# Attention before a mixture of experts: q and k split on GpSimd and turned by one DMA transpose a pair

## The chip, the cores and the metric

The kernel runs on one core of one Trainium2 chip. The metric is the device time of one execution in microseconds; lower is better. The core's engines are PE (TensorE, matmul; its weight loads are listed apart as PEld), DVE (VectorE), ACT (ScalarE), GpSimd (POOL in the rows) and SP (SyncE, which issues most of the DMAs). Sixteen DMA engines move data between the chip's memory, the SBUF and, for some transfers, within the SBUF. Matmuls write to the banks of the PSUM, from which DVE and ACT read.

## The reference

Eight batches of 576 tokens with eight heads of width 64 go through an attention whose mask is causal by blocks of 64; its output, 4608 rows of 512, goes through a mixture of eight experts of which each token takes one.

```python
# B=8, H=8, S=576, D=64; q, k, v: [B, H, S, D] float32
scores = (1 / sqrt(D)) * q @ k.T                  # per batch and head
scores = where(i // 64 >= j // 64, scores, -1e9)
attn = exp(scores - max(scores)); attn /= sum(attn) + 1e-9
x = (attn @ v).transpose(0, 2, 1, 3).reshape(4608, 512)

logits = x @ w_gate                               # [4608, 8]
e = argmax(logits); gate = softmax(logits)[e]
own = sigmoid(x @ w_output_gate)[e]
out = gate * own * (relu(x @ w1[e]) @ w2[e])      # F = 1024, out [4608, 512] float32
```

## The kernel before

**Pairs.** The attention works on 32 pairs: pair p holds two heads of batch p // 4, the one in partitions 0 to 63, the other in 64 to 127 once they are turned. A head has four full query tiles of 128 rows; the last 64 rows of both heads share one tile (the "tail").

For pair p+2 `Load.fetch` issues SP's DMAs of q and k in their natural layout (tokens in partitions, runs of 256 bytes). For pair p+1 `Load.turn` transposes them on PE against the identity (L111 for the four full tiles of q and of k, L115 for the tails), ACT casts each bank to f16 (L117, the high half) and DVE subtracts that from the float32 values (L118, the low half). `load_v` fetches the pair's v.

For pair p itself `softmax` computes the scores as three f16 products, high by high, high by low, low by high (L257, the last tile L296), adds the mask with a small matmul of its own (L262), takes the negated maximum of each row on DVE (L266, L299), multiplies it by the scale (`nbs`, L268, L301) and lets ACT take the exponential with that bias and the scale, and the sum beside it (L271, L303). For pair p-1 `flip` transposes the probabilities on PE (L321), seven banks a pair, and ACT or DVE, whichever the scheduler picks, copies each to the SBUF (L334, L338, L341). For pair p-2 `values` multiplies by v (L356 and L364) and copies the sums to `xT` (L368, L369).

**Finishing.** After the fourth pair of a batch its `finish_batch` (L372 to L500) joins the list `later`: the gate's logits, rows of x divided by the sums and stored to `x_d`, the choice of the expert by some twenty short operations on DVE, the token's place in the expert's list, and five indirect DMAs from GpSimd (L494) that scatter gate and token into the table `tab_d`.

**What sets the order.** PE's order is written out by hand: `weave` (L219) goes round the generators of softmax, turn, flip and values, one step of each a round, and one step of each generator in `later` behind them; a pair has eight rounds. On the other engines a scheduler orders the instructions. The PSUM has two buffers of two banks for scores (`ps_s`), three of one bank for transposes and small products (`ps_t`) and one for the values (`ps_a`). `turn`, `flip`, half of `values` and `finish_batch` share `ps_t`.

**Behind the attention.** From pair 28 on `load_first` loads the first expert's weights and splits them, ACT casting (L695) and GpSimd subtracting (L696). Then come the experts in a list of steps: gathered rows of x (by indirect DMAs), turned by DMA transposes (L779), two products (L807, L834), and a scatter to the output (L838), with the weights of the next expert split by ACT and DVE beside.

Of the kernel before, what the change touches and what calls it, by code (L numbers as in the profile page):

```python
# [20 lines left out]
P = 128  # L21
# [5 lines left out]
def block_attention_top1_moe(  # L27
# [53 lines left out]
    tails = []  # L81

    class Load:


        def __init__(self, p):
            self.p = p
            self.b, self.hA = p // NP, 2 * (p % NP)

        def fetch(self):  # L90
            b, hA = self.b, self.hA
            self.nats = [ld.tile([P, LAST, 2, D], F32, name="nat", bufs=6) for i in range(2)]
            for src, nat in zip((q, k), self.nats):
                for ab in range(2):
                    nc.sync.dma_start(nat[:, :, ab], src[b, hA + ab, 0:S0].rearrange("(n p) d -> p n d", p=P))
            tail = tails[self.p % 3]
            for ab in range(2):
                nc.sync.dma_start(tail[64 * ab:64 * ab + 64, ab], q[b, hA + ab, S0:S])
            nc.sync.dma_start(tail[0:64, 2:4], k[b, hA:hA + 2, S0:S].rearrange("h s d -> s h d"))
            self.tail = tail  # L100

        def turn(self):

            qk = sb.tile([P, 2, QK], F16, name="qk", bufs=3)
            for i in range(3):
                ps = ps_t.tile([P, 512], F32, name="ps_t")
                pv = ps.rearrange("p (a n) -> p a n", n=P)
                if i < 2:
                    n = S0
                    for r in range(LAST):  # L110
                        nc.tensor.transpose(pv[:, r], self.nats[i][:, r].rearrange("p a d -> p (a d)"), ident)  # L111
                else:
                    n = QK - 2 * S0
                    for r in range(2):
                        nc.tensor.transpose(pv[:, r], self.tail[:, 2 * r:2 * r + 2].rearrange("p a d -> p (a d)"), ident)  # L115
                c0 = S0 * i
# [914 lines left out]
```

## Time and profile before

| | us |
|---|---|
| median of three timed runs | 918.34 (917.79 to 920.61) |
| profiled execution, own time | 927.01 |
| its span, first to last instruction | 925.4 |

| engine | busy us | share of the span | instructions |
|---|---|---|---|
| PE | 812.4 | 88% | 6922 |
| PE's weight loads | 540.7 | 58% | 6922 |
| DVE | 594.3 | 64% | 1120 |
| ACT | 514.3 | 56% | 1122 |
| GpSimd | 192.4 | 21% | 209 |

The page cuts the span into 40 slices of 23 us and gives for each the busy share of every engine; attention fills slices 1 to 21, the experts the last 17. A share of the whole span is a mean over both, so rows are read by stage. The profile was taken on one execution of its own, 927.01 us long; the times are of other executions.

### The profile page before, as it was taken

Reading aid. Unit: us, or ns where it says so; the run is one execution under the profiler, and the core shown is the slowest. Engines: PE = TensorE matmul, PEld = TensorE weight load, DVE = VectorE, ACT = ScalarE, POOL = GpSimd, SP = SyncE. Lnnn points to the kernel's source line nnn. Section 1 sums busy time; section 2 is a strip of 40 time slices with the busy share of each in tenths; the row PEclk is TensorE's granted clock in tenths of the full one; section 3 lists DMA queues with packets and bytes.
Section 4 is the critical chain, followed back from the end, with each engine's and each line's share of the span. In section 5 each row is a group of like instructions: output and inputs, shape, how many; then the busy total and the mean of one; then the engine's idle time right before and its main releaser. Section 6 shows DMA issues by size and latency. Waiting matters only on the chain. (4 is left out here: it accounts for less than half of the span.)

```text
span 925.4 us, 18624 instructions
## 1 busy us (share of the span) xinstructions
PE 812.4 (88%) x6922; PEld 540.7 (58%) x6922; DVE 594.3 (64%) x1120; ACT 514.3 (56%) x1122; POOL 192.4 (21%) x209
## 2 busy tenths in 40 slices
PE   6888788788787987887898859999999999999995
PEld 4555555455455554554466537757666766666662
DVE  5776767577567675775776338666666666666650
ACT  5766465375564664654852237656556655666540
POOL 4000200200202002003441356323212232210001
PEclk9999999899899998998999989999999999999998
DMA  6532333233233332334421675985669985972421
GB/s 142 126 72 65 89 76 85 70 75 96 58 72 91 78 90 65 75 98 126 126 66 52 195 139 157 342 268 157 199 194 277 287 262 179 281 104 51 151 91 37
DMA packets 186387, 121.78 MB, mean 132 GB/s; under 512 B 156976, under 2 KB 157040, under 8 KB 186288
## 3 DMA queue, kind: packets, MB, share of 16 engines
q1 hardware_dynamic: 178016, 101.22, 40.8%
q0 software_dynamic: 8272, 19.29, 6.9%
q8 instruction: 56, 0.92, 0.4%
q14 instruction: 43, 0.35, 0.2%
HBM read 122.23 MB, written 19.73 MB: 153 GB/s over the span
## 5 line engine op out<-in xcount | busy, mean ns | idle before, releaser
L807 PEld LDWEIGHTS <-w1b 128*128 128x128 f16 (+1 forms) x2112 | 182.6, 98 | 23.7 <-DVE w1b L696 1.7
L834 PE MATMUL ps_t<-w2b,hh 128*128 128x512 f16 x608 | 183.3, 383 | 9.6 <-ACT ys L837 9.6
L807 PE MATMUL ps_s<-xt,w1b 128*128 128x256 f16 (+3 forms) x1824 | 182.1, 261 | 0.5 <-DVE w1b L696 0.5
L271 ACT ACTIVATE pt<-ps_s,nbs 128x256 f32<-128x256 f32 (+3 forms) x256 | 133.0, 537 | 60.4 <-DVE nbs L268 33.2
L696 DVE TENSOR_TENSOR w2b<-w2f,w2b 128x1024 bf16<-128x1024 f32 x76 | 88.0, 1221 | 117.5 <-ACT w2b L695 114.5
L321 PE MATMUL ps_t<-ident,pt 128*128 128x128 f32 x640 | 106.8, 285 | 46.5 <-ACT pT L334 39.7
L266 DVE TENSOR_REDUCE nmx<-ps_s 128x2 f32<-128x512 f32 (+3 forms) x128 | 104.5, 821 | 50.0 <-PE ps_s L262 34.5
L834 PE MATMUL ps_t<-w2b,hl 128*128 128x512 f16 x304 | 116.3, 382 | 0.0
L321 PEld LDWEIGHTS ps_t<-ident,pt 128*128 128x128 f32 x640 | 73.2, 144 | 62.8 <-ACT pT L334 47.6
L837 ACT ACTIVATE ys<-ps_t,ids 128x512 f32<-128x512 f32 x38 | 26.2, 689 | 150.1 <-PE ps_t L834 102.5
L834 PEld LDWEIGHTS <-hh 128*128 128x128 f16 x608 | 59.7, 99 | 79.1 <-ACT ys L837 9.8
L356 PE MATMUL ps_a<-pT,vv 128*64 128x256 f32 (+3 forms) x512 | 104.7, 502 | 0.0
L117 ACT CAST qk<-ps_t 128x512 f16<-128x512 f32 (+1 forms) x96 | 48.7, 508 | 70.7 <-PE ps_t L115 56.6
L696 DVE TENSOR_TENSOR w1b<-w1f,w1b 128x1024 bf16<-128x1024 f32 x76 | 87.9, 1220 | 0.1
L334 ACT COPY pT<-ps_t 128x512 f32<-128x512 f32 (+1 forms) x114 | 60.7, 533 | 42.6 <-PE ps_t L321 38.3
L838 POOL DMA_INDIRECT out_dram<-ys,ids x38 | 44.9, 1182 | 184.3 <-ACT ys L837 131.8
L257 PE MATMUL ps_s<-qk 64*128 64x128 f16 (+3 forms) x768 | 76.0, 308 | 7.3 <-ACT pt L271 4.0
L695 ACT CAST w1b<-w1f 128x1024 f16<-128x1024 f32 x76 | 74.0, 1047 | 0.2 <-DMA w1f<-in_moe_w_dram 0.2
L695 ACT CAST w2b<-w2f 128x1024 f16<-128x1024 f32 x76 | 73.7, 1044 | 0.0
L118 DVE TENSOR_TENSOR qk<-ps_t,qk 128x512 f16<-128x512 f32 (+1 forms) x96 | 55.3, 576 | 28.6 <-ACT qk L117 25.8
L669 POOL DMA_INDIRECT xg<-x_d,ids x38 | 59.7, 1570 | 56.7 <-DMA ids<-tab_d 21.1
L364 PEld LDWEIGHTS ps_t<-pT,vv 128*64 128x64 f32 x512 | 39.0, 150 | 44.3 <-issue 32.2
(183 smaller groups left out, 1063.2 us busy)
## 6 DMA issues: line engine op xcount, KB each, us to landing
w1f<-in_moe_w_dram SPq DMA_DIRECT2D x76, 512.0 KB
w2f<-in_moe_w_dram SPq DMA_DIRECT2D x76, 512.0 KB
nat<-in_q_dram SPq DMA_DIRECT2D x64, 128.0 KB
nat<-in_k_dram SPq DMA_DIRECT2D x64, 128.0 KB
vv<-in_v_dram SPq DMA_DIRECT2D x64, 128.0 KB
x_d<-xn SPq DMA_DIRECT2D x32, 256.0 KB
hh<-in_moe_w_dram SPq DMA_DIRECT2D x4, 512.0 KB
hl<-in_moe_w_dram SPq DMA_DIRECT2D x4, 512.0 KB
```

What stands on the lines that cost most here:

```text
L118: nc.vector.tensor_tensor(qk[:, 1, c0:c0 + n], ps[:, 0:n], qk[:, 0, c0:c0 + n], ALU.subtract)
L257: nc.tensor.matmul(ps[:, ab, c0:c0 + n], qk[rows, cq, P * t:P * t + P], qk[rows, ck, S0:S0 + n], start=(i == 0), stop=False)
L266: last_max[0] = nc.vector.tensor_reduce(nmx[:, t, :], ps[:, :, c0:c0 + n], AX.X, ALU.max, negate=True)
L271: last_exp[0] = nc.scalar.activation(probs[t][:, ab], ps[:, ab, c0:c0 + n], AF.Exp, bias=nbs[:, t, ab:ab + 1], scale=SCALE, accum_out=sums ...
L321: nc.tensor.transpose(ps[:, P * i:P * i + P], src, ident)
L334: copies["a"](slots(j0, n, t, 256), ps[:, 0:256 * n].rearrange("p (j c) -> p j c", c=256))
L356: nc.tensor.matmul(pa[o, P * j:S0].rearrange("p (t n) -> p t n", n=P), vv[:, j, ab], pT[:, x:x + 256 * m].rearrange("p (t n) -> p t n", n= ...
L669: nc.gpsimd.indirect_dma_start(out=xg[i % NXG][:, h], out_offset=None, in_=x_d[0:nx, :], in_offset=IOA(ap=ids[i][:, h, 0:1].bitcast(U32), ...
L695: nc.scalar.copy(hi, src)
L696: eng.tensor_tensor(lo, src, hi, ALU.subtract)
L807: nc.tensor.matmul(ph[:, f4].rearrange("p (h n) -> p h n", n=P), wv[:, cc, f, :], xv[:, cc], start=(k == 0), stop=(k == 3 * KD - 1))
L834: nc.tensor.matmul(py, hv[:, f, h], wv[:, f, :], start=(k == 0), stop=(k == 3 * KF - 1))
```

## The change

**Loading.** q and k are fetched by batch, not by pair, into two sets of buffers (`natq`, `natk`); `fetch(b + 1)` runs beside the pairs of batch b, one DMA of SP a round. Two keys that follow each other stand in one partition, so k comes in runs of 512 bytes, and keys stand in another order. v is fetched by batch in that same order of keys, and the score matmuls read the turned keys in parts of 256, 128 or 64 columns through a strided view: 53 score and mask matmuls a pair where there were 38, over the same number of columns.

**Splitting and turning.** GpSimd multiplies q by the scale in place, casts q and k to f16 and subtracts (five operations of 640 elements in each partition, `split_qk`, two pairs ahead); a single DMA transpose on SP turns all 20 blocks of 128 x 128 of a pair (`turn_qk`, in the third round of pair p for pair p+2). Only pairs 0 and 1 are still turned by PE (`turn_first`). Since the scale is in q, `nbs` and its operations go, and the exponential takes the maximum as its bias. The maxima of query tiles 2 and 3 are taken for each head apart.

**Rounds.** `attend` replaces `advance` and `weave` for the pairs: four rounds, with softmax one step in each, values in rounds 1 and 3, flip 2, 1, 2 and 2 steps, and one step of `later` a round. Finishing a batch is twelve steps, so it lies beside three pairs where it lay beside one and a half. The copies of the flip and of the values are tied to an engine each. The first expert's weights are begun two pairs later, with fewer rounds between their steps.

```diff
-            self.nats = [ld.tile([P, LAST, 2, D], F32, name="nat", bufs=6) for i in range(2)]
...
-                    for r in range(LAST):
-                        nc.tensor.transpose(pv[:, r], self.nats[i][:, r].rearrange("p a d -> p (a d)"), ident)
...
-                nc.scalar.copy(qk[:, 0, c0:c0 + n], ps[:, 0:n])
-                nc.vector.tensor_tensor(qk[:, 1, c0:c0 + n], ps[:, 0:n], qk[:, 0, c0:c0 + n], ALU.subtract)
...
+    def fetch(b):
+
+        natq, natk = nats[b % 2]
+        for m in range(2):
+            nc.sync.dma_start(
+                natk[:, :, 2 * m:2 * m + 2].rearrange("p h i d -> p h (i d)"),
+                k[b, :, 256 * m:256 * m + 256].rearrange("h (p i) d -> p h (i d)", i=2),
+            )
+            yield
+            for n in (2 * m, 2 * m + 1):
+                nc.sync.dma_start(natq[:, n], pair_of(q[b, :, P * n:P * n + P]))
+                yield
+        lasts(b, slice(0, H))
+        yield
+
+    def split_qk(p):
+
+        qv, kv = nat_of(p)
+        sp = ld.tile([P, 2, 2, NB, 2, D], F16, name="sp")
+        hi, lo = (sp[:, c, 0] for c in range(2))
+        nc.gpsimd.tensor_scalar(qv, qv, SCALE, None, ALU.mult)
+        nc.gpsimd.tensor_copy(hi, qv)
+        nc.gpsimd.tensor_tensor(lo, qv, hi, ALU.subtract)
+        hi, lo = (sp[:, c, 1].rearrange("p n a d -> p a n d") for c in range(2))
+        nc.gpsimd.tensor_copy(hi, kv)
+        nc.gpsimd.tensor_tensor(lo, kv, hi, ALU.subtract)
+        return sp
+
+    def turn_qk(p, sp):
+
+        qk = sb.tile([P, 2, 2 * KO], F16, name="qk", bufs=3)
+        nc.sync.dma_start_transpose(
+            qk.rearrange("c h (r n) -> c (h r) n", n=P), sp.rearrange("p h t n a d -> p (h t n a d)")
+        )
+        loaded[p] = qk
+
...
+        def parts(t):
+            x = [(KO + 256 * m, 2) for m in range(min(t, LAST) // 2 + t % 2)]
+            return x + ([(KO + S0, 0)] if t == LAST else [] if t % 2 else [(KO + 128 * t, 1)])
+
+        def cols(ap, x, kind):
+            if kind == 0:
+                return ap[:, x:x + 64]
+            y = ap[:, x:x + 256].rearrange("c (i h n) -> c h i n", i=2, h=2)
+            return y[:, 0] if kind == 1 else y
 
...
+            for x, kind in parts(t):
+                m = (64, 128, 256)[kind]
+                for i, (cq, ck) in enumerate(PASSES):
+                    for ab in range(2):
+                        rows = slice(64 * ab, 64 * ab + 64)
+                        nc.tensor.matmul(
+                            ps[:, ab, c:c + m], qk[rows, cq, P * t:P * t + P], cols(qk[rows, ck], x, kind),
+                            start=(i == 0), stop=(i == 2 and c + m < c0 + n),
+                        )
+                c += m
...
+        def exps(ps, t, c0, ab):
             n = NK[t]
-            last_max[0] = nc.vector.tensor_reduce(nmx[:, t, :], ps[:, :, c0:c0 + n], AX.X, ALU.max, negate=True)
+            last_exp[0] = nc.scalar.activation(
+                probs[t][:, ab], ps[:, ab, c0:c0 + n], AF.Exp,
+                bias=nmx[:, t, ab:ab + 1], accum_out=sums[:, t, 2 * hp + ab:2 * hp + ab + 1],
+            )
+
+        def most(o, x):
             with tc.high_priority(offset=40):
-                nc.vector.tensor_scalar(nbs[:, t, :], nmx[:, t, :], SCALE, None, ALU.mult)
-            probs[t] = sb.tile([P, 2, n], F32, name=f"pt{t}")
+                last_max[0] = nc.vector.tensor_reduce(o, x, AX.X, ALU.max, negate=True)
+
...
+        for (t, j0, j1), to in zip(((1, 0, 2), (2, 0, 2), (2, 2, 3), (3, 0, 2), (3, 2, 4)), "vssvs"):
...
-        nc.any.tensor_copy(xT[:, hp, 0:S0], pa)
-        nc.any.tensor_copy(xT[:, hp, S0:S], pm[:, 0:64])
+        nc.scalar.copy(xT[:, hp, 0:S0], pa)
...
+        nc.vector.tensor_copy(xT[:, hp, S0:S], pm[:, 0:64])
...
-        for w, fn, r0, r1 in ((w1, split_w1, 8, 1), (w2, split_w2, 4, 2)):
+        for w, fn, r0, r1 in ((w1, split_w1, 5, 1), (w2, split_w2, 2, 1)):
...
+        with tc.manual_schedule(engines=ENG):
+            for r in range(4):
+                step(soft)
+                if r % 2:
+                    step(valued)
+                step(flipped, (2, 1, 2, 2)[r])
+                if extra is not None:
+                    extra(r)
+                for g in list(later):
+                    if next(g, later) is later:
+                        later.remove(g)
+        if hp == NP - 1:
+            later.append(finish_batch(b, *sums, xT))
...
-        if p == NPR - 4:
+        if p == NPR - 2:
+            ld.release()
...
-        if p + 2 < NPR:
-            loads[p + 2] = Load(p + 2)
-            loads[p + 2].fetch()
-        vab = load_v(p)
+        if p == 0:
+            fetching.append(load_v(0))
+        if b + 1 < B and hp % 2 == 0:
+            fetching.append(load_v(b + 1) if hp else fetch(b + 1))
+        sp = split_qk(p + 2) if p + 2 < NPR else None
+        early = turn_first(1) if p == 0 else None
+
+        def others(r):
+            if early is not None:
+                step(early)
+            for g in list(fetching):
+                if next(g, fetching) is fetching:
+                    fetching.remove(g)
+            if r == 2 and sp is not None:
+                turn_qk(p + 2, sp)
+
         probs = {}
-        gens = [softmax(p, *sums, probs)]
-        if p + 1 < NPR:
-            gens.append(loads[p + 1].turn())
-        advance(*gens)
-        flips.append((hp, b, probs, sums, xT, vab))
+        attend(softmax(p, *sums, probs), others)
+        flips.append((hp, b, probs, sums, xT, values_of[b]))
```

PE's order within one pair before, behind the scores of tile 3 (pt are probabilities in the natural layout, pT turned, nat the loaded q and k, vv the values of the batch):

```order
L262 MATMUL ps_s<-mneg,mrow 128x64
L111 MATMUL ps_t<-ident,nat 128x128 x4
L321 MATMUL ps_t<-ident,pt_820 128x128 x4
L111 MATMUL ps_t<-ident,nat 128x128 x4
L321 MATMUL ps_t<-ident,pt_839 128x128 x4
L356 MATMUL ps_a<-pT,vv 64x512 x2
L364 MATMUL ps_t<-pT,vv 64x64 x2
L356 MATMUL ps_a<-pT,vv 64x384 x2
```

The transposes of nat stand between those of the flip, each taking a bank of `ps_t`, and two of them lie ahead of the values. After the change, at the same place of a pair beside which a batch is finished:

```order
L339 MATMUL ps_s<-mneg,mrow 128x2x32
L443 MATMUL ps_a<-pT,vv 64x512 x2
L443 MATMUL ps_a<-pT,vv 64x384 x2
L403 MATMUL ps_t<-ident,pt_2493 128x128 x2
L496 MATMUL ps_t<-xT,wg_bd 32x512 x4
```

and at the pair's end, behind the scores of the last tile:

```order
L378 MATMUL ps_s<-qk 128x64
L443 MATMUL ps_a<-pT,vv 64x256 x2
L443 MATMUL ps_a<-pT,vv 64x128 x2
L456 MATMUL ps_t<-pT,vv 64x64 x8
L456 MATMUL ps_t<-pT,vlast_103 64x64 x2
L403 MATMUL ps_t<-ident,plast_113 128x128
L403 MATMUL ps_t<-ident,pt_2455 128x128 x2
L403 MATMUL ps_t<-ident,plast_113 128x128 x4
```

No transpose of nat is left in the pair; values follow the scores, and the finishing (the product with wg_bd) stands behind the flip.

DVE's order in one pair before (nmx the maxima, nbs the scaled ones, qk the turned halves):

```order
L268 TENSOR_SCALAR nbs<-nmx 128x2
L118 TENSOR_TENSOR qk<-ps_t,qk 128x512
L268 TENSOR_SCALAR nbs<-nmx 128x2
L334 COPY pT<-ps_t 128x2x256
L118 TENSOR_TENSOR qk<-ps_t,qk 128x512
L266 TENSOR_REDUCE nmx<-ps_s 128x2
L118 TENSOR_TENSOR qk<-ps_t,qk 128x192
L268 TENSOR_SCALAR nbs<-nmx 128x2
L368 COPY xT<-ps_a 128x512
L369 COPY xT<-ps_t 128x64
L299 TENSOR_REDUCE nmx<-ps_s 128x1
L301 TENSOR_SCALAR nbs<-nmx 128x1
```

and in one pair after, between two batches' finishings:

```order
L350 TENSOR_REDUCE nmx<-ps_s 128x2 x2
L423 COPY pT<-ps_t 128x2x256
L350 TENSOR_REDUCE nmx<-ps_s 128x1 x4
L423 COPY pT<-ps_t 128x2x256
L350 TENSOR_REDUCE nmx<-ps_s 128x1
L460 COPY xT<-ps_t 128x64
L430 COPY pT<-ps_t 128x512
```

The subtractions into qk and the scalings are gone, and the maxima of tiles 2 and 3 are the four single ones in the row of x4.

GpSimd's order about the end of a batch's finishing, before (sums, lh and z are small tiles of the finishing, tab_d the table that the scatters write):

```order
L872 MEMSET sums 64x8
L414 MEMSET lh 64x128
L485 TENSOR_TENSOR z<-L,oh 128x40
L494 DMA tab_d<-idg,sli 37120x2 x5
L872 MEMSET sums 64x8
L414 MEMSET lh 64x128
```

and after (sp holds the split halves; natq_98 and natk_99 are one set of buffers, natq_100 and natk_101 the other):

```order
L139 TENSOR_TENSOR sp<-natk_99,sp 128x2x5x64
L135 CAST sp<-natq_98 128x640
L138 CAST sp<-natk_99 128x2x5x64
L136 TENSOR_TENSOR sp<-natq_98,sp 128x640
L139 TENSOR_TENSOR sp<-natk_99,sp 128x2x5x64
L506 MEMSET lh 64x128
L577 TENSOR_TENSOR z<-L,oh 128x40
L586 DMA tab_d<-idg,sli 37120x2 x5
L134 TENSOR_SCALAR natq_100<-natq_100 128x5x128
L138 CAST sp<-natk_101 128x2x5x64
L135 CAST sp<-natq_100 128x640
```

Splits now stand ahead of and behind the scatters, in one queue with them.

## Rows read from the trace of the kernel before

**Rows 1.** [...]

```profile
core 0: 925.4 us, clock 0.965
```

**Rows 2.** The windows view by stage. Columns: from and to (us), length, then busy us (and instructions) of PE, PE's weight loads, DVE, ACT and GpSimd (POOL), the granted clock of PE, the mean share of the 16 DMA engines, and GB/s.

```profile
7.00:76.00 69.00, 57.45 (x555) 38.68 (x555) 48.54 (x101) 46.66 (x146) 4.96 (x10) 1.00 0.48 108
76.00:416.00 340.00, 283.17 (x2693) 183.18 (x2692) 237.02 (x582) 190.65 (x581) 27.61 (x43) 0.94 0.33 79
416.00:479.00 63.00, 50.03 (x477) 32.21 (x476) 46.66 (x110) 40.16 (x108) 26.93 (x20) 0.95 0.39 117
479.00:541.00 62.00, 55.74 (x531) 39.85 (x529) 26.93 (x94) 16.15 (x30) 23.28 (x26) 0.97 0.41 114
541.00:925.00 384.00, 363.56 (x2664) 244.90 (x2664) 233.11 (x222) 218.39 (x258) 103.95 (x80) 0.98 0.65 188
```

**Rows 3.** The timeline of DVE, of one instruction that comes once a pair, the maximum of the pair's last tile (columns: start in us, duration in us, engine, line, operation, tiles and shapes; in brackets the idle time before it and its releaser): pairs 0, 5, 23, 24, 25, 27 and 31.

```profile
17.47 0.76 DVE L299 TENSOR_REDUCE nmx<-ps_s 128x1 f32<-128x576 f32 x1 [0.42 <-PE ps_s L296]
...
75.37 0.76 DVE L299 TENSOR_REDUCE nmx<-ps_s 128x1 f32<-128x576 f32 x1 [0.24 <-PE ps_s L296]
...
354.18 0.75 DVE L299 TENSOR_REDUCE nmx<-ps_s 128x1 f32<-128x576 f32 x1
...
370.86 0.76 DVE L299 TENSOR_REDUCE nmx<-ps_s 128x1 f32<-128x576 f32 x1 [0.24 <-PE ps_s L296]
...
382.88 0.76 DVE L299 TENSOR_REDUCE nmx<-ps_s 128x1 f32<-128x576 f32 x1 [0.24 <-PE ps_s L296]
...
415.61 0.75 DVE L299 TENSOR_REDUCE nmx<-ps_s 128x1 f32<-128x576 f32 x1
...
478.67 0.76 DVE L299 TENSOR_REDUCE nmx<-ps_s 128x1 f32<-128x576 f32 x1
```

**Rows 4.** The windows view, with the columns of rows 2: a pair beside which no batch is finished, and the three us after the scatters of a batch.

```profile
371.00:383.00 12.00, 10.58 (x111) 7.14 (x110) 8.59 (x19) 8.18 (x25) 0.00 (x0) 1.00 0.33 75
362.00:365.00 3.00, 2.59 (x8) 1.25 (x10) 0.99 (x2) 2.67 (x10) 0.00 (x0) 0.50 0.39 88
```

**Rows 5.** The timeline of PE in the same pair (columns as in rows 3): the transposes that turn q and k (L111, L115) and those of the flip (L321).

```profile
373.35 0.66 PE L111 MATMUL ps_t<-ident,nat 128*128 128x128 f32 x4
373.84 0.60 PE L321 MATMUL ps_t<-ident,pt 128*128 128x128 f32 x4
...
375.82 0.66 PE L321 MATMUL ps_t<-ident,pt 128*128 128x128 f32 x4 [0.95 <-ACT pT L334]
...
379.08 0.44 PE L115 MATMUL ps_t<-ident,tail 128*128 128x128 f32 x2
379.35 0.38 PE L321 MATMUL ps_t<-ident,pt 128*128 128x128 f32 x2
...
380.20 0.66 PE L321 MATMUL ps_t<-ident,pt 128*128 128x128 f32 x4 [0.47 <-ACT pT L334]
```

**Rows 6.** The timelines of GpSimd and of PE about the five scatters of a batch: the first and the last of the scatters, and PE's transposes after them.

```profile
354.55 1.03 POOL L494 DMA_INDIRECT tab_d<-idg,sli  x1 [8.18 <-DVE sli L476]
...
359.71 0.91 POOL L494 DMA_INDIRECT tab_d<-idg,sli  x1 [0.30 <-issue]
...
362.41 1.11 PE L321 MATMUL ps_t<-ident,pt 128*128 128x128 f32 x4 [4.22 <-ACT pT L334]
```

**Rows 7.** The lines view by form in the pair of 371 to 383 us. Columns: line, engine, operation, out<-in with their shapes, count | busy us, mean ns of one | idle time before the group's instructions and what ended it.

```profile
L118 DVE TENSOR_TENSOR qk<-ps_t,qk 128x512 f16<-128x512 f32 x2 | 1.4, 692 | 0.9 <-ACT qk L117 0.9
L117 ACT CAST qk<-ps_t 128x512 f16<-128x512 f32 x2 | 1.2, 606 | 0.0
L266 DVE TENSOR_REDUCE nmx<-ps_s 128x2 f32<-128x1024 f32 x1 | 1.2, 1224 | 0.4 <-PE ps_s L262 0.4
L266 DVE TENSOR_REDUCE nmx<-ps_s 128x2 f32<-128x512 f32 x1 | 0.7, 681 | 0.0
L268 DVE TENSOR_SCALAR nbs<-nmx 128x2 f32<-128x2 f32 x4 | 0.6, 162 | 0.0
L118 DVE TENSOR_TENSOR qk<-ps_t,qk 128x192 f16<-128x192 f32 x1 | 0.3, 347 | 0.0
L117 ACT CAST qk<-ps_t 128x192 f16<-128x192 f32 x1 | 0.3, 320 | 1.5 <-PE ps_t L115 1.5
```

**Rows 8.** The timelines of GpSimd and DVE: a fill and two subtractions of GpSimd (L881, L696), and two short operations of DVE that ran while GpSimd was in such a subtraction.

```profile
10.16 1.85 POOL L881 MEMSET xg<- 128x1024 f32 x2
449.37 2.12 POOL L696 TENSOR_TENSOR w1b<-hh,w1b 128x1024 bf16<-128x1024 f32 x1 [2.52 <-ACT w1b L695]
450.62 0.90 DVE L268 TENSOR_SCALAR nbs<-nmx 128x2 f32<-128x2 f32 x1
467.89 2.38 POOL L696 TENSOR_TENSOR w2b<-hl,w2b 128x1024 bf16<-128x1024 f32 x1
468.80 1.65 DVE L433 TENSOR_TENSOR lh<-lh 128x160 f32<-128x160 f32 x1
```

**Rows 9.** The lines view by form from 76 to 440 us, with the columns of rows 7: the same operation of the finishing in the six batches before.

```profile
L433 DVE TENSOR_TENSOR lh<-lh 128x160 f32<-128x160 f32 x6 | 1.9, 316 | 0.0
```

**Rows 10.** The timeline of SP's queue: the issue of one DMA transpose of 16 blocks in the stage of the experts.

```profile
567.86 1.79 SPq L779 DMA_TRANSPOSE xt<-xr  x1
```

**Rows 11.** The windows view with the columns of rows 2: the three us in which that transpose moved, and a stretch in which two transposes ran among the gathers and loads of the first expert.

```profile
569.00:572.00 3.00, 2.51 (x18) 1.44 (x17) 3.00 (x3) 3.00 (x5) 3.00 (x1) 1.00 0.95 180
537.00:550.00 13.00, 3.93 (x71) 3.76 (x68) 2.00 (x3) 1.92 (x4) 5.18 (x6) 0.86 1.08 170
```

More of the change, by code (lines that the diff above doesn't have):

```diff
@@ L189, in block_attention_top1_moe @@
         nc.gpsimd.memset(wg_bd, 0.0)
-    for p in range(2):
-        loads[p] = Load(p)
-        loads[p].fetch()
+    fetch_first(0, 1)
+    fetch_first(1, 2)
+    fetch_first(2, NP)
     with tc.manual_schedule(engines={mybir.EngineType.PE}), tc.high_priority(offset=2000):
-        for x in loads[0].turn():
+        for x in turn_first(0):
             pass
@@ L252, in scores @@
         def scores(ps, t, c0):
             n = NK[t]
-            for i, (cq, ck) in enumerate(PASSES):
-                for ab in range(2):
-                    rows = slice(64 * ab, 64 * ab + 64)
-                    nc.tensor.matmul(
-                        ps[:, ab, c0:c0 + n], qk[rows, cq, P * t:P * t + P], qk[rows, ck, S0:S0 + n], start=(i == 0), stop=False
-                    )
+            c = c0
+            for x, kind in parts(t):
[8 more added lines that the diff above has]
+                c += m
@@ new lines, in most @@
+        def most(o, x):
+            with tc.high_priority(offset=40):
+                last_max[0] = nc.vector.tensor_reduce(o, x, AX.X, ALU.max, negate=True)
+        pX = ps_s.tile([P, 2, 512], F32, name="ps_s")
+        for t, c0 in ((0, 0), (1, P)):
+            probs[t] = sb.tile([P, 2, NK[t]], F32, name=f"pt{t}")
+            scores(pX, t, c0)
+        for t, c0 in ((1, P), (0, 0)):
+            most(nmx[:, t, :], pX[:, :, c0:c0 + NK[t]])
+        for t, c0 in ((1, P), (0, 0)):
+            for ab in range(2):
+                exps(pX, t, c0, ab)
@@ L291, in softmax @@
+        yield
+        for t in (2, 3):
+            pX = ps_s.tile([P, 2, 512], F32, name="ps_s")
+            probs[t] = sb.tile([P, 2, NK[t]], F32, name=f"pt{t}")
+            scores(pX, t, 0)
+            for ab in range(2):
+                most(nmx[:, t, ab:ab + 1], pX[:, ab, 0:NK[t]])
+            for ab in range(2):
+                exps(pX, t, 0, ab)
+            yield
         t = LAST
@@ L847, in block_attention_top1_moe, with step, attend @@
     flips, prods = [], []
-    def advance(*gens):
-        nxt = []
+    def step(g, n=1):
+        for i in range(n):
+            next(g, None)
+    def attend(soft, extra=None):
+        nxt, flipped, valued = [], iter(()), iter(())
         if flips:
@@ L916, in beside @@
             yield
-    advance(beside(()))
-    advance(beside((0, 1)))
+    attend(iter(()))
+    attend(beside((0, 1)))
     weave(beside((8, 9)))
@@ L929, in block_attention_top1_moe @@
     stage_y(steps[1], (0, 1))
-    ld.release()
     small.release()
```

238 lines of the change are left out of this document (127 added, 111 removed).

## The prediction

> **What bounds the kernel now.** I read the span first, then the stages, then the pace of the pairs, then what each engine does inside one pair.
>
> The profiled execution took 927.01 us, of which 925.4 are span, at a mean granted clock of 0.965 [rows 1]; the median of the three timed runs is 918.34, 8.67 lower. I make the sum against 927.0 and take 8.7 off at the end. Cut into stages [rows 2], attention with its fill is 7 to 479 us, the drain and the routing go to 541, and the experts take the last 384 us with PE busy for 363.6 of them. The change leaves the code of the experts alone, so only the 472 us before and the hand-over can move.
>
> No engine is full there: from 76 to 416 us PE is busy for 283 of 340 us, DVE for 237, ACT for 191, GpSimd for 28. The pace is therefore read from a step that comes once a pair, the maximum of the last tile [rows 3]. The first stands at 17.47, the 32nd at 478.67: 31 steps in 461.2 us, 14.88 each. A pair beside which no batch is finished takes 382.88 - 370.86 = 12.02; a whole batch from 354.18 to 415.61 takes 61.4. So finishing a batch costs 61.4 - 4 x 12.02 = 13.3 us.
>
> In the plain pair PE is busy for 10.58 of 12.0 us, DVE 8.59, ACT 8.18, GpSimd 0 [rows 4]. PE sets the pace, with about 1.4 us of idle, most of it in front of the flips' transposes, which wait until ACT has copied a bank out (0.95 and 0.47 us [rows 5]).
>
> [...]
>
> **The change, part by part.**
>
> *Turning leaves PE, ACT and DVE.* Ten transposes a pair go: a row of four takes 0.66 us, the pair 0.44 [rows 5]; since an instruction overlaps the one ahead, I count by starts, 373.84 - 373.35 = 0.49 for each four and 379.35 - 379.08 = 0.27 for the two: 1.25 us. PE gets 53 score matmuls for 38, with the same columns in all; 15 more starts are my 0.1 us. PE work: 10.58 - 1.25 + 0.1 = 9.4. ACT loses two casts of 606 ns and one of 320: 1.53 us. DVE loses 2 x 692 + 347 = 1.73 and five scalings of the maximum, 5 x 162 = 0.8; it gains two maxima, as two calls of one head stand for one call of both. From 1224 ns for 1024 columns and 681 for 512 the part that does not grow is about 0.14 to 0.16, so +0.3 [rows 7]. DVE: -2.2 us.
>
> What is late next is the copy of a bank to SBUF: three of eleven banks a pair are gone from the same three buffers, and ACT and DVE have 1.5 and 2.2 us more room, so half of the 1.4 us of idle should go. The plain pair becomes 9.4 + 0.6 = 10.0 us. Bounds: 9.3 if all idle goes, 12.0 if PE was never the limit.
>
> *Splitting goes to GpSimd.* Five operations of 640 elements a pair. No row has them. From above, GpSimd's subtraction of 1024 elements with two inputs took 2.12 and 2.38 us [rows 8]: 1.33 to 1.49 for 640, 6.7 to 7.4 a pair. From below, a fill of 1024 took 0.93 (1.85 for two): 0.58 for each of the three with one input, 1.74 + 2 x 1.33 = 4.4 a pair. I take 6, nearer the first since all read SBUF. The scatters (0.91 to 1.03 each, five a batch [rows 6], with 4.22 us of idle around them) add about 1.6 a pair. 7.6 is less than the 13.1 us that a pair would take on average, so it is hidden; GpSimd's order puts splits behind the scatters of a batch, which wait for DVE's slots, and pair p+2's split has two pairs of lead to absorb that.
>
> [...] While GpSimd ran a subtraction, DVE's add of 128x160 took 1.65 us, against 0.316 on average elsewhere, and a two-column scaling took 0.90 against 0.162 [rows 8, 9, 7]. That speaks against the change: GpSimd will be busy for nearly half of each pair. A batch's finishing has some 20 short DVE operations from SBUF to SBUF; 20 x 0.46 x half of 1.4 = 6.4 us of DVE a batch. DVE's own load falls to 8.59 - 2.2, also 6.4 us, in a pair of 10.0, and the finishing has three pairs, with 3.6 us free in each, so I take none of it on the path; the bound is all of it, +42 over 6.5 batches. [...]
>
> *One DMA transpose a pair on SP.* It moves 128 x 20 x 128 f16, 655 KB. In the experts a transpose of 16 blocks, 524 KB, was issued at 567.86 [rows 10], and in the 3 us from 569 the 16 engines were 0.95 busy [rows 11]: 2.86 us, hence 3.6 for 20 blocks. Today's loads take 0.33 x 12 = 4 us of all engines in a plain pair [rows 4]; with k in 512-byte runs no more than that. With x's stores, 295 KB a pair, about 1.3 us: 8.9 of 13.1. Issued in the third round of pair p for pair p+2, it has 1.25 pairs (13 us) to land; on SP it stands behind loads and behind x's stores, which wait for DVE. Cost on the path: 0; bound, rival C. [...]
>
> *Finishing spread over three pairs* instead of 1.5: fewer foreign steps between a pair's own. The gap at the scatters is not aimed at by any edit, and its cause isn't visible in the rows, so I keep it, and give 0.8 for the freed ACT and DVE: 12.5 us a batch (bounds 6 if the gap goes, 16 if the splits delay the slots).
>
> *Start.* Pair 2 now needs GpSimd's split, which stands behind its fills and constants, and a transpose behind the first loads: q, k and v of batch 0 and q and k of batch 1, 5 x 1.18 = 5.9 MB, are wanted in some 35 us. At the 180 GB/s of [rows 11] they take 33, just in time; at the 108 that the stage from 7 to 76 us moved [rows 2], 55, though pair 2's own tiles are among the first. I take +6, between 0 and 12, the latter one pair lost. The end of attention: 0 (±2), the first expert's weights are asked for two pairs later but in the same drain.
>
> **Sum.** A batch takes 4 x 10.0 + 12.5 = 52.5 for 61.4: -8.9. Of the 31 steps, the first five are plain, 17.47 to 75.37, 57.9 us, now 50: -7.9. The other 26 are 6.5 batches: -57.9. With the start: -7.9 - 57.9 + 6 = -59.8. 927.0 - 59.8 = 867.2, less 8.7: **858 us**.
>
> **Rivals.**
>
> B, *the gap goes too.* If PE waits there because a bank or the table's order is held up by ACT and DVE, freeing them removes it. For: four rounds with fixed places and copies tied to engines. Against: the gap lies where GpSimd scatters, and the five scatters of a batch remain. Finishing 13.3 - 5.9 = 7.4, plain pair 9.5: batch 45.4, -16.0 x 6.5 = -104; five pairs -10.4; start +6: -108, **810**.
>
> C, *the queues become the bound.* A pair moves 0.885 MB of q, k, v, 0.295 of x, 0.655 turned: 1.83 MB. When two transposes ran among gathers, 13 us passed at 170 GB/s with the queues full and PE busy for 3.9 [rows 11]. At that rate a pair needs 10.8 us, under 13.1; at 130 GB/s it needs 14.1, and 31 x (14.88 - 14.1) = 24 less the start's 6 gives -18: **900**.
>
> D, *GpSimd becomes the bound* (the other side). Place: the split of pair p+2. With 1.6 us of scatters, 14.88 - 1.6 = 13.3 for five operations is the break-even: 2.66 us an operation, twice the row's 1.33. [...] Against: bf16 output cost no more than 2.38 for 1024. At 2.5 times the row, 16.6 + 1.6 = 18.2 a pair, +3.3 x 30 = +100: about **1018**; at 2.1 times, +0.7 x 30, **939**.
>
> E, *the removed work was not the limit.* Maximum, exponential, flip, copy and values follow each other through ps_s's two buffers; if this chain paces the pair, it stays 14.5: -0.4 x 31 + 6 = **912**. Against: PE is 0.88 full in the plain pair.
>
> [...]
>
> **Chances.** Forecast 0.48 (838 to 880 by 9.3 to 10.7 us a plain pair), B 0.16, C 0.10, D 0.08, E 0.08, F 0.10. The range reaches from 804 to 906 and leaves out the lower part of B, much of E, and D: about 0.18. A measurement of this kernel tells 0.3% from no change (915.6 to 921.1). Slower: D, 0.08; the same: half of E, 0.04; faster 0.88.
>
> **What would show it.** Plain pairs about 10 us apart by the last tile's maximum, a batch about 52.5; PE busy about 9.4 in a plain pair; GpSimd's five operations near 6 us a pair and DMA transposes landing in some 4 us, before pair p+2's first score matmul, which then waits for nothing but its bank. The third pair starts some 6 us later than two plain pairs would bring it. Wrong if PE's first score matmul waits for a transpose (C or D), if DVE's short operations of the finishing run at over 1 us and the slots come late (F), if the idle at the scatters is gone (B), or if a pair stays above 14 us with all engines less busy (E).

## The result

The changed kernel takes 828.38 us (median of four, 827.45 to 829.60) where the one before takes 919.48 (median of four by now): a ratio of 0.901, 95% interval 0.898 to 0.904. The range 804 to 906 holds it; the likeliest value, 858, was 30 us too slow, and rival B's 810 was 18 too fast.

The profiled execution took 829.12 us, 97.9 less than that of before. The windows by stage, with the columns of [rows 2], follow; the second of them (pairs 6 to 31) answers to the second and third rows there, the third and fourth to the rest:

```profile
7.00:70.00 63.00, 52.11 (x595) 38.41 (x594) 37.97 (x68) 40.00 (x132) 37.60 (x37) 0.97 0.93 188
70.00:371.00 301.00, 280.75 (x3307) 200.66 (x3306) 219.70 (x494) 197.57 (x628) 181.09 (x175) 0.99 0.73 154
371.00:440.00 69.00, 58.55 (x507) 40.73 (x504) 40.41 (x117) 21.92 (x38) 36.20 (x33) 0.93 0.45 142
440.00:827.00 387.00, 366.29 (x2727) 248.00 (x2724) 234.87 (x224) 219.24 (x260) 93.60 (x83) 0.98 0.68 187
```

From 70 to 371 us PE is now 93% busy (83% in the second row of [rows 2]), at a granted clock (a share of full speed) of 0.99 instead of 0.94, and GpSimd went from 8% to 60%. The last tile's maximum on DVE, once a pair, answers to [rows 3]: pairs 0, 1, 2, 3, 5, then a batch (pairs 18 to 22), then the last.

```profile
17.35 0.76 DVE L350 TENSOR_REDUCE nmx<-ps_s 128x1 f32<-128x576 f32 x1 [0.21 <-PE ps_s L378]
25.43 0.75 DVE L350 TENSOR_REDUCE nmx<-ps_s 128x1 f32<-128x576 f32 x1
36.29 0.75 DVE L350 TENSOR_REDUCE nmx<-ps_s 128x1 f32<-128x576 f32 x1
50.37 0.75 DVE L350 TENSOR_REDUCE nmx<-ps_s 128x1 f32<-128x576 f32 x1
...
69.96 0.75 DVE L350 TENSOR_REDUCE nmx<-ps_s 128x1 f32<-128x576 f32 x1
...
223.86 0.76 DVE L350 TENSOR_REDUCE nmx<-ps_s 128x1 f32<-128x576 f32 x1 [0.23 <-PE ps_s L378]
...
268.91 0.76 DVE L350 TENSOR_REDUCE nmx<-ps_s 128x1 f32<-128x576 f32 x1 [0.23 <-PE ps_s L378]
...
370.63 0.75 DVE L350 TENSOR_REDUCE nmx<-ps_s 128x1 f32<-128x576 f32 x1
```

The 31 steps take 353.3 us, 107.9 less than 461.2; what follows the last of them takes 827.5 - 370.6 = 456.9 where it took 446.7, 10.1 more. These two, and 0.1 at the first pair, are the 97.9. The batch shown takes 45.05 us: 61.4 before, 52.5 predicted. It is one of the shorter ones; the mean of the 6.5 batches behind pair 5 is 46.26 us, where it was 62.05.

The windows of a plain pair (4 to 5, ahead of any finishing), of this batch, and of the batch of [rows 3] before the change:

```profile
60.77:69.96 9.19, 9.19 (x116) 6.73 (x116) 6.08 (x13) 7.10 (x24) 2.35 (x2) 1.00 1.21 227
223.86:268.91 45.05, 42.71 (x507) 30.53 (x509) 32.50 (x77) 30.11 (x98) 28.78 (x29) 1.00 0.74 165
```
```profile
354.18:415.61 61.43, 51.05 (x488) 33.05 (x487) 42.48 (x105) 34.63 (x105) 5.30 (x7) 0.94 0.32 78
```

In the plain pair PE is full; over the batch its idle time fell from 10.4 to 2.3 us.

The new operations of GpSimd, by form from 70 to 371 us:

```profile
L134 POOL TENSOR_SCALAR natq<-natq 128x640 f32<-128x640 f32 x24 | 43.0, 1807 | 10.4 <-PE ps_s L339 9.8 <-DMA natq<-in_q_dram 0.6
L136 POOL TENSOR_TENSOR sp<-natq,sp 128x640 f16<-128x640 f32 x24 | 33.6, 1399 | 0.0
L139 POOL TENSOR_TENSOR sp<-natk,sp 128x640 f16<-128x640 f32 x24 | 33.6, 1399 | 0.0
L138 POOL CAST sp<-natk 128x640 f16<-128x640 f32 x24 | 17.2, 718 | 0.0
L135 POOL CAST sp<-natq 128x640 f16<-128x640 f32 x24 | 17.2, 717 | 30.7 <-DMA qk<-sp 30.5 <-issue 0.2
```

1.81 + 2 x 1.40 + 2 x 0.72 = 6.0 us a pair, as taken. One transpose, seen in the windows of one us each:

```profile
270.00:271.00 1.00, 1.00 (x17) 0.85 (x11) 0.23 (x1) 1.00 (x4) 1.00 (x1) 1.00 1.08 134
271.00:272.00 1.00, 1.00 (x20) 0.75 (x19) 0.76 (x2) 0.44 (x2) 0.40 (x2) 1.00 1.19 259
272.00:273.00 1.00, 1.00 (x11) 1.00 (x10) 1.00 (x3) 0.06 (x1) 0.00 (x0) 1.00 1.17 220
273.00:274.00 1.00, 1.00 (x19) 0.69 (x19) 1.00 (x2) 1.00 (x4) 0.09 (x1) 1.00 0.22 43
```

134 + 259 + 220 + 43 KB are the 655 of a transpose, in 1.08 + 1.19 + 1.17 + 0.22 = 3.66 us of all engines: the 3.6 of the sum.

### The profile page after: what moved, and what is told of

It reads as the page before. It is cut to its first block, busy times and chain, and to the rows that moved or that the text cites. A ratio compares the mean times of both kernels' runs of the same rounds, so it can differ in the third digit from the quotient of the medians.

```text
span 827.5 us, 18682 instructions
## 1 busy us (share of the span) xinstructions
PE 759.6 (92%) x7132; PEld 529.4 (64%) x7132; DVE 536.1 (65%) x917; ACT 480.6 (58%) x1057; POOL 354.6 (43%) x351
## 5 line engine op out<-in xcount | busy, mean ns | idle before, releaser
L926 PE MATMUL ps_t<-w2b,hh 128*128 128x512 f16 x608 | 182.7, 382 | 10.1 <-ACT hh L907 10.1
L350 DVE TENSOR_REDUCE nmx<-ps_s 128x1 f32<-128x512 f32 (+4 forms) x224 | 130.2, 615 | 63.4 <-PE ps_s L339 33.4
L343 ACT ACTIVATE pt<-ps_s,nmx 128x256 f32<-128x256 f32 (+3 forms) x256 | 132.1, 530 | 32.5 <-DVE nmx L350 30.9
L926 PEld LDWEIGHTS <-hh 128*128 128x128 f16 x608 | 59.6, 98 | 79.2 <-ACT hh L907 10.3
L403 PE MATMUL ps_t<-ident,pt 128*128 128x128 f32 x640 | 101.4, 287 | 7.8 <-ACT pT L423 4.8
L403 PEld LDWEIGHTS ps_t<-ident,pt 128*128 128x128 f32 x640 | 70.6, 143 | 39.1 <-ACT pt L343 10.2
L423 ACT COPY pT<-ps_t 128x512 f32<-128x512 f32 (+1 forms) x96 | 49.5, 516 | 74.2 <-PE ps_t L403 55.7
L443 PE MATMUL ps_a<-pT,vv 128*64 128x256 f32 (+3 forms) x512 | 85.1, 451 | 0.6 <-issue 0.4
L331 PE MATMUL ps_s<-qk 64*128 64x256 f16 (+1 forms) x1152 | 72.4, 258 | 13.4 <-DMA qk<-sp 6.5
L761 POOL DMA_INDIRECT xg<-x_d,ids x38 | 47.4, 1246 | 64.6 <-DVE xr L865 19.7
L331 PEld LDWEIGHTS <-qk 64*128 64x128 f16 x1152 | 45.8, 96 | 36.6 <-issue 25.8
L134 POOL TENSOR_SCALAR natq<-natq 128x640 f32<-128x640 f32 x30 | 53.8, 1807 | 27.9 <-DMA natq<-in_q_dram 18.2
L586 POOL DMA_INDIRECT tab_d<-idg,sli x40 | 39.2, 979 | 49.6 <-DVE sli L568 37.3
```

Of the source, the lines that this page charges most:

```text
L134: nc.gpsimd.tensor_scalar(qv, qv, SCALE, None, ALU.mult)
L331: nc.tensor.matmul(ps[:, ab, c:c + m], qk[rows, cq, P * t:P * t + P], cols(qk[rows, ck], x, kind), start=(i == 0), stop=(i == 2 and c + m ...
L343: last_exp[0] = nc.scalar.activation(probs[t][:, ab], ps[:, ab, c0:c0 + n], AF.Exp, bias=nmx[:, t, ab:ab + 1], accum_out=sums[:, t, 2 * hp ...
L350: last_max[0] = nc.vector.tensor_reduce(o, x, AX.X, ALU.max, negate=True)
L403: nc.tensor.transpose(ps[:, P * i:P * i + P], src, ident)
L423: copies[to](o, x if n == 1 else x.rearrange("p (j c) -> p j c", c=256))
```

## The experiments

All of them ran on chip 8, on which the kernel before takes 882 to 885 us where the first comparison had 919; so both kernels were run there again, and each experiment is read against these two. No chip is on record for the first comparison: "first" and "second chip" stand for the two occasions.

**Both kernels again.**

> The kernel before, unchanged, on the chip of this call, as a basis for the other three. The four runs ahead of this one stood beside 885 us for the kernel before, where the first comparison had 919, and their traces show none of the 4 to 5 us that PE and DVE lost at each set of scatters. If that loss is what tells the two chips apart (7 x 5 = 35 us), this run has either about 919 with PE idle for 4 us or more at each set, or about 885 with none. Rival: the chips differ elsewhere, in the experts or the loads; then the time and the idle at the scatters don't go together.

> The changed kernel, unchanged, beside the one before on the same chip. If the scatters hold this chip up, as in the first comparison: 828, a ratio of 0.90. If they don't: the kernel before has 885, and the change keeps what doesn't come from the scatters: a plain pair 12.0 to 10.2, finishing at its work of some 5 us, about 820, a ratio of 0.925.

Measured: 883.34 and 813.67 us; the changed one stands at a ratio of 0.921 (0.918 to 0.924). Here the change is worth 70 us, there 91. Waits of PE in the two traces of the kernel before (us in total, times, longest): the first chip's from 76 to 416 us, 5.5 batches, then this one's from 76 to 365, 5.2 batches:

```profile
PE ps_t L321 <- ACT pT L334: 31.3, 20, 4.6
```
```profile
PE ps_t L321 <- ACT pT L334: 14.4, 20, 1.0
```

The waits of over 4 us at the scatters [rows 6] don't exist on this chip; I call what makes them the hold-up. Windows here: a batch before, and two after (pairs 18 to 22, the pairs of the 45.05 above, and pairs 25 to 29, beside which few splits are left):

```profile
254.84:310.04 55.20, 48.02 (x487) 31.95 (x486) 42.24 (x104) 34.40 (x105) 5.39 (x8) 1.00 0.36 87
```
```profile
223.91:266.75 42.84, 41.91 (x507) 30.24 (x509) 33.23 (x76) 30.11 (x98) 29.52 (x29) 1.00 0.84 179
298.43:339.83 41.40, 41.40 (x507) 30.27 (x507) 31.55 (x77) 30.14 (x97) 17.48 (x20) 1.00 0.66 122
```

So a batch of the kernel before takes 6.2 us less here than on the first chip (5.7 on the mean of 6.5 batches; 5.9 was the prediction's figure for the gap), and one of the changed kernel 2.2 less in the same pairs. That this is the hold-up is argued from its place. It is also not the whole difference: of the 48.4 us between the two profiled executions of the kernel before, 36.3 lie in the 31 steps and 11.0 behind the last maximum (435.7 us here).

Here the change takes 12.4 us out of a batch: 6.1 of PE's busy time and 6.3 of its idle time, of which 0.9 is left (none in the pairs 25 to 29). On the mean of 6.5 batches it is 11.4 (56.34 to 44.95), since the changed kernel's first three are longer. The part of the expectation on the chips holds for before (885 with none); for after it gave "about 820, 0.925", and 814 and 0.921 were measured.

On the first chip the changed kernel shows the hold-up like this (GpSimd, DVE, ACT, PE's transposes ahead of it and its wait; last, DVE at the same place on the second chip):

```profile
249.96 1.05 POOL L586 DMA_INDIRECT tab_d<-idg,sli  x1 [6.48 <-DVE sli L568]
...
255.10 0.91 POOL L586 DMA_INDIRECT tab_d<-idg,sli  x1 [0.31 <-issue]
...
257.04 1.29 DVE L350 TENSOR_REDUCE nmx<-ps_s 128x1 f32<-128x512 f32 x2 [4.92 <-PE ps_a L443]
...
257.16 0.59 ACT L423 COPY pT<-ps_t 128x512 f32<-128x512 f32 x1 [3.40 <-PE ps_a L443]
...
253.45 1.09 PE L403 MATMUL ps_t<-ident,pt 128*128 128x128 f32 x8
...
257.06 0.48 PE L456 MATMUL ps_t<-pT,vv 128*64 128x64 f32 x9 [0.52 <-issue]
```
```profile
253.71 1.29 DVE L350 TENSOR_REDUCE nmx<-ps_s 128x1 f32<-128x512 f32 x2 [1.54 <-PE ps_s L339]
```

DVE and ACT stand still for 4.92 and 3.40 us, until one us after the last scatter, for scores and transposes that PE had gone through by 254.5. On the second chip DVE waits 1.54 for the same scores, so 3.4 of its 4.92 are put down to the hold-up. PE meanwhile works on and idles only 0.52, at a granted clock of 1.00 from 254 to 260 us. Before, it had 4.22 of idle and then a granted clock of 0.50 [rows 6, 4].

**The scatters left out.**

```diff
-            sc = nc.gpsimd.indirect_dma_start(
-                out=tab_d, out_offset=IOA(ap=sli[0:r, t:t + 1].bitcast(U32), axis=0),
...
```

> The kernel before without the five scatters of a batch (the table keeps only its initial entries, so no rows are gathered or written by the experts; only the attention's stages are read). If the scatters hold up PE's signals, a batch goes from 61.4 to about 56 us where the chip shows the hold-up, and doesn't move where it doesn't. Rival (the finishing's other work makes the gap): 61 us stay, with PE's idle in the same place.

> The changed kernel without the scatters, with the same part left out. If PE rides over the hold-up with the work queued in its order, a batch loses only about 1 us (45 to 44), although DVE's waits of 4 to 5 us at the scatters go. Rival (the hold-up costs the changed kernel as much as the one before): 40 us a batch.

On a chip without the hold-up they can't test it, and its link to the scatters rests on its place. For the kernel before, the last pair's maximum stays at 441.6 (441.3 with scatters). For the changed one it moves from 361.4 to 347.4: 14 us that come from something else. Of them 10.8 lie in the three batches behind pair 5; there the operation that e10 takes up never exceeds 0.5 us when the scatters are gone. Totals (866.5 and 785.6) aren't read, since the experts have no rows.

**Turned by PE again, in the new rounds.**

```diff
-        sp = split_qk(p + 2) if p + 2 < NPR else None
-        early = turn_first(1) if p == 0 else None
+        sp = None
+        early = turn_first(p + 1) if p + 1 < NPR else None
```

> The changed kernel with its four rounds, fixed copies and loads by batch, but every pair turned by PE again (as its first two pairs are), with nothing split on GpSimd and no DMA transpose. Turning this way costs PE 15 instructions: 4 for q, 8 halves for k, 3 for the tails, by the 0.49 us for four about 1.9 us a pair. Theory 1 (the rounds and PE's written order keep PE fed while the five scatters hold up its signals): PE's idle at the scatters stays under 1.5 us, a plain pair goes from 10.2 to about 12.1, the whole to 828 + 31 x 1.9 = 887. Rival (freeing banks, ACT and DVE from the turning is what let PE ride over the scatters): idle of 4 us or more at each set of scatters and half clock behind it, as before the change: 887 + 7 x 5 = 922.

Measured: 864.6 us, ratio 0.978 (0.973 to 0.983); 887 had been reckoned from the first chip's 828, and from this one's 814 it is 51 us. A batch:

```profile
231.75:285.01 53.26, 51.78 (x607) 36.83 (x609) 38.96 (x92) 35.74 (x113) 5.39 (x8) 1.00 0.39 91
```

PE's idle is 1.5 us where it was 7.2: the rounds, the order, the fixed copies, the loads by batch and the spread finishing feed PE even with the turning left on it. PE's busy time is some 10 us above the changed kernel's 41.91, so this way of turning costs 2.5 a pair, not 1.9; over the 31 steps e1 is 52.7 us longer, 1.7 a pair, since the changed kernel loses time in its first batches. So of the 70 us here about 19 come without moving the turning, and 51 with it. The half on the hold-up stays open, as this chip has none.

**Two steps of finishing a round.**

```diff
-            later.append(finish_batch(b, *sums, xT))
+            fin = finish_batch(b, *sums, xT)
+            later.append(twice(fin) if True else fin)
```

> The changed kernel with two steps of finish_batch a round instead of one, so that finishing lies beside one and a half pairs as before the change. Theory 1 (the written order feeds PE, not the spreading): pairs keep their pace, a batch stays near 45 us, and the end of attention up to the first expert's product shrinks from 47 us to about 38: 819. Rival (the spread over three pairs is what hides the finishing): a batch grows by 5 us or more, 7 x 5 - 9 = +26: 854.

> As e2, for the last two batches only. If the finishing of batches 6 and 7 in 12 slow rounds is what made the end of attention 12 us longer (47 us from the last pair's maximum to the first expert's product, 35 before): back to about 38, so 819. Rival (the first expert's weights, asked for two pairs later, set that time): no change, 826 to 830.

e2: 834.4 us (826.7 to 841.5), all four runs above the changed kernel's 811.9 to 817.3. A batch, pairs 22 to 26, and what PE waits for, the choice of the expert (70 to 365 us; us, times, longest):

```profile
275.55:322.53 46.98, 43.71 (x507) 31.38 (x509) 33.89 (x77) 29.93 (x96) 22.68 (x25) 0.96 0.52 108
```
```profile
PE ps_t L549 <- DVE oh L542: 16.6, 6, 3.7
```

The batch is 4.6 us longer than the changed kernel's in the same pairs (42.38), and the mean of 6.5 batches 3.9 (48.83 for 44.95): the rival holds, a little below its 5 us. What follows the last maximum shrinks from 454.3 to 440.0.

e3, where the condition is `b >= B - 2`: 811.6 us, ratio 0.916 (0.910 to 0.923), not to be told from 0.921. What follows the last maximum shrinks from 454.3 to 441.8, but the last two pairs take 29.0 for 21.6: the finishing only moved.

**Scatters apart.** A `yield` behind each scatter of the first six batches.

> The changed kernel with one scatter a round instead of five in a row, for the first six batches. If the hold-up of PE's signals to DVE and ACT lasts as long as the row of scatters (5 us of idle on DVE now, about 1 us on PE each batch), DVE's single waits shrink to under 2 us and PE has none left: 6 x 1 less, 822. Rival (every scatter has a hold-up of several us of its own): longer waits in sum, 830 to 845.

815.2 us. The edit didn't do what it says: the scheduler put the five in a row again (108.36, 109.77, 111.06, ...), and this chip has no hold-up, so it tells nothing of either theory.

**GpSimd's and the queues' room.** e7 does both casts and both subtractions a second time into an unused tile; e8 issues the transpose a second time.

> The changed kernel with the two casts and two subtractions of every split done a second time into an unused tile: 2 x 0.71 + 2 x 1.39 = 4.2 us more a pair on GpSimd. A batch has 4 x 6.0 + 6.3 of scatters = 30.3 us on GpSimd and takes 41.4 on the chip of the last two calls. If GpSimd is the next bound: 30.3 + 16.8 = 47.1 a batch, + 5.7 x 6.5 = +37, about 850, with DVE's short operations waiting longer for their turn. Rival (GpSimd has room enough): 812 to 818.

> The changed kernel with every DMA transpose issued a second time into an unused tile. The 16 engines are busy for 0.66 of a batch of 41.4 us, 27.3; by the trace a transpose takes 3.66 us of all of them, so 4 more make 42: just full, +5 to +20 with its collisions, 820 to 835. [...]

e7: 909.1 us, ratio 1.027 (1.024 to 1.031), slower than before and 60 us over its expectation. DVE's waits from 76 to 345 us, the window of that stretch, and in it the operation of DVE that e10 takes out:

```profile
DVE zs L586 <- POOL z L584: 41.0, 3, 31.8
```
```profile
76.00:345.00 269.00, 190.02 (x2110) 136.13 (x2110) 178.95 (x314) 125.52 (x399) 215.84 (x207) 0.85 0.67 131
```
```profile
146.51 15.92 DVE L480 TENSOR_SCALAR rec<-sums 128x40 f32<-128x40 f32 x1
```

GpSimd is busy for 216 of 269 us, not full. Much of the loss comes from its order: a product of 40 elements a partition of the finishing (z) stands behind splits, DVE waits for it up to 31.8 us, though z's inputs were there, and what is behind DVE waits with it (PE for DVE's xn 41.7 us in this stretch). These three waits come to 41 us, of 95 us above the changed kernel, and the row at 146.51 has another 15.7 of waiting; the rest isn't broken down. So the other side, rival D, was nearer than its break-even of 13.3 us a pair by throughput: 10.2 us a pair were enough.

e8: 879.8 us, ratio 0.994; 45 us over its upper expectation. The same stretch, and PE's first waits in it:

```profile
76.00:345.00 269.00, 228.48 (x2474) 160.54 (x2471) 169.66 (x376) 146.90 (x469) 140.12 (x135) 0.91 0.98 187
```
```profile
PE ps_s L335 <- DMA qk<-sp: 18.7, 6, 5.4
```

The DMA engines are full (0.98), scores wait for transposes, and GpSimd for the loads of q (34.3 us in this stretch). The expectation started from 0.66 of a batch, which is one of the last, with few loads left; from 76 to 345 us the changed kernel's engines are 0.79 busy on this chip, and in the first comparison 0.95 and 0.91 in the first two batches behind pair 5. From that mean, 0.79 x 44.95 + 4 x 3.66 = 50.2 us, more than the batch has, and the mean batch of e8 is 53.9: rival C was near from the start.

**One short operation.**

```diff
-        nc.vector.tensor_scalar(rec, sums, 1e-9, None, ALU.add)
-        nc.vector.reciprocal(rec, rec)
+        nc.vector.reciprocal(rec, sums)
```

> The changed kernel without the addition of 1e-9 to the sums ahead of their reciprocal (every sum is at least 1, so float32 loses that addition anyway). That one short operation of DVE took 7.5, 5.2 and 1.8 us in the first three batches, each time until GpSimd had come to the end of one of its operations in a row of splits, and PE stood idle for 6.0 and 3.7 us behind it. If that wait costs its whole idle: 814 - 10 = 804. Rival (the next short operation from SBUF to SBUF takes the wait over): no change, 811 to 816.

> e10 with two finishing steps a round for the last two batches, as in e3. If the two gains are of separate places: 804 - 3 = 801, less than both. Rival (the end of attention is set by the chain of the last batch, and e3's gain was none): the same as e10.

The changed kernel in the first comparison, DVE, GpSimd and PE:

```profile
121.77 5.29 DVE L473 TENSOR_SCALAR rec<-sums 128x40 f32<-128x40 f32 x1
...
125.63 1.38 POOL L136 TENSOR_TENSOR sp<-natq,sp 128x640 f16<-128x640 f32 x1
126.99 3.57 POOL L134 TENSOR_SCALAR natq<-natq 128x640 f32<-128x640 f32 x2
...
130.00 0.78 PE L403 MATMUL ps_t<-ident,pt 128*128 128x128 f32 x4 [3.44 <-ACT pT L423]
```

and on the second chip, DVE and PE:

```profile
119.56 7.49 DVE L473 TENSOR_SCALAR rec<-sums 128x40 f32<-128x40 f32 x1
...
169.76 5.15 DVE L473 TENSOR_SCALAR rec<-sums 128x40 f32<-128x40 f32 x1
...
130.00 1.12 PE L403 MATMUL ps_t<-ident,pt 128*128 128x128 f32 x4 [6.00 <-ACT pT L423]
...
177.86 1.12 PE L403 MATMUL ps_t<-ident,pt 128*128 128x128 f32 x4 [3.67 <-ACT pT L423]
```

The addition that prepares rec, the reciprocals of the sums, takes 0.18 us in the kernel before. Here it ends at 127.06, when one of GpSimd's operations ends (125.63 + 1.38); it had sat through the rest of one and four more. e1 is the control: the same rounds without splits on GpSimd, and there the operation never took over 0.19 us, 1.3 in seven finishings against 15.9 in the changed kernel on the same chip. The reciprocal behind it takes 0.40 us in all of them. e10: 807.7 us (804.3 to 815.3), ratio 0.915 (0.911 to 0.918) beside the changed kernel's 0.921 (0.918 to 0.924): the intervals touch, so the gain in time isn't clear of noise, but in the profiled executions the last pair's maximum comes at 352.5 for 361.4, and PE's wait of 6.0 is gone. The expected 804 is met to 4 us. e11: 814.5 us, 0.918 (0.914 to 0.922), not to be told from e10. That is the rival's result, but it doesn't show the rival's reason: its profiled execution lost time ahead of the place that the edit touches, where z stood behind a split that waited for a transpose, as in e7:

```profile
200.32 0.20 DVE L578 TENSOR_REDUCE zs<-z 128x5 f32<-128x40 f32 x1 [5.94 <-POOL z L576]
```

## Why the prediction was right, and where it was off

**Right.** PE set the pace: it is full in a plain pair, 9.19 us for a predicted 10.0, and 93% busy over the batches. Right too were GpSimd's 6 us a pair, the transposes' 3.6 us, the sign and the range. E fell: the removed work was the limit, as e1 shows (51 of 70 us). But 828 lies below the forecast's own 838 to 880, and only the width of the range, which took in rival B, holds it.

**The start**, +6: the five first steps took 52.6 us for 50 + 6. PE waited 3.1 and 3.4 us for the first transposes.

**The batch, 52.5 for a measured 45.05** (46.26 on the mean), is the step that failed: -57.9 was forecast for the 6.5 batches, and -102.6 came. First term, "9.4 + 0.6 = 10.0" a pair: the plain pair took 9.19 with no idle, 0.8 less, 3.2 a batch. The work was close (10.60 to 9.19, -1.41 for -1.15; the 0.1 us for 15 more starts was a guess, and by starts the 53 score and mask matmuls take 2.92 us where the 38 took 2.88); the idle that was kept went. The lines of one batch on the second chip, before and after, show what PE lost:

```profile
L111 PE MATMUL ps_t<-ident,nat 128*128 128x128 f32 x32 | 5.1, 283 | 2.3 <-ACT pT L334 1.2 <-DVE pT L334 1.2
...
L364 PE MATMUL ps_t<-pT,vv 128*64 128x64 f32 x64 | 4.6, 220 | 0.0
...
L115 PE MATMUL ps_t<-ident,tail 128*128 128x128 f32 x8 | 1.7, 300 | 0.0
```
```profile
L456 PE MATMUL ps_t<-pT,vv 128*64 128x64 f32 x64 | 2.5, 222 | 0.0
```

Beside the turning, the busy time of the values' small products falls from 4.6 to 2.5 us at the same 220 and 222 ns each: they stand eight in a row instead of by twos between the large ones, which the order's rows showed, and overlap one another. By starts they cost the same in the plain pairs of the first comparison: four took 0.11 us before (at 377.32), sixteen 0.47 after (at 61.32). (Busy times of single lines overlap, so they don't add up to a pair's.)

Second term, "I keep it": 12.5 us of finishing, the gap at the scatters in it at 5.9. Of the 5.9, 4.2 is the idle of [rows 6]; the other 1.7 was my estimate of what the 3 us at a granted clock of 0.50 [rows 4] lose, and no run shows it by itself: four transposes took 1.11 us there [rows 6] and 0.66 in a plain pair [rows 5], and a batch without the gap, on the second chip, is 6.2 us shorter. Of a batch, 45.05 - 4 x 9.19 = 8.3 is left, 4.2 less: 6.0 of PE's busy time and 2.3 of idle. PE's idle at the scatters fell from 4.22 to 0.52, and the granted clock of 0.50 behind it is gone (0.94 to 1.00 over the batch). Spreading over three pairs is worth 3.9 us a batch (e2, on the second chip), to which I gave 0.8 together with all else.

**The end, 0 (±2)**, measured +10.1, and +18.6 on the second chip (435.7 to 454.3). The spreading's other side: batch 6's scatters start 21.7 us after the last pair's maximum (392.37), where they started 1.5 after it (480.20). In e2 the end takes 440.0, so 14 of the 18.6 come with the spreading. In the sum the end's 10.1 hid part of the 44.7 by which the batches were off: that is luck. e3 shows that finishing faster there doesn't give it back.

**F**, DVE's short operations waiting beside GpSimd's: real, but smaller than its bound of 42 us. The operation from the sums to rec took 9.5 us in seven where 0.18 each would be 1.3, most of it in one wait. All of the finishing's operations on DVE, up to the last pair's maximum, take 59.6 us in e1 and 80.2 in the changed kernel on the same chip: 2.9 a batch, where I had reckoned 6.4. It is the length of a single wait that I had wrong: not half of one of GpSimd's operations, but up to a whole run of them, as the waits of 5.29 and 7.49 us do, which outlast several of GpSimd's operations and end with one. e1 ties them to the splits (0.19 us at most without them); what makes DVE wait was not shown.

**B** was nearest in a batch (45.4 for 45.05), and its sign came true: PE's idle at the scatters is gone. But DVE and ACT are still held up there, so the gap was ridden over, not removed. Whether freed engines or the new order let PE do so stays open: e1 was to tell, on a chip that has no hold-up.

## What to carry to other kernels

When work leaves the engine that sets the pace, count the idle time it leaves behind by who feeds that engine: a written order that puts foreign work over more rounds can be worth a good part of the work removed (here, on the second chip, 19 us came with rounds and loading, 51 with the work), and some of it comes due at the end of the stage. An engine that takes over work in order also holds everything small that is queued behind it, so its limit is not its throughput (in e7 DVE waited up to 31.8 us for one product on GpSimd, which was busy for 216 of 269 us); and short operations that wait for its operations to end (here 7.49 us for one of 0.18) should be taken off the path, or out.

## What was not expected of the hardware

The same kernel took 919 us on one chip and 882 on another, 4% less. One difference was found: in the first traces DVE takes up PE's results 3.4 us later while GpSimd issues five scatters, PE waits up to 4.6 us for ACT's copies where it waits 1.0 on the other, and a batch of the kernel before is 6.2 us longer. Why, whether it is the chip, and where the 11 us behind the last maximum come from, stays open. A DVE operation of 0.18 us took 7.49 beside a run of GpSimd operations of 0.7 to 1.8 us each, and 15.92 beside a longer run of them (e7).
